# The turn from first to second stage of a two-level Strassen-Winograd kernel: where C11's last tile is squared, and where the first small product's sums stand

## The chip, the cores and the metric

The kernel runs on one core of one Trainium2 chip. The metric is the device time of one execution in microseconds (us), taken as a median of runs. The engines are called PE (TensorE's matmuls; PEld is its weight loads), DVE (VectorE), ACT (ScalarE), POOL (GpSimd) and SP (SyncE, which issues most transfers).

## The reference

```python
kv  = einsum('bhsd,bhse->bhde', k, v)           # 8 batches, 8 heads, 576 rows, 64 wide
out = einsum('bhsd,bhde->bhse', q, kv)
rms = sqrt(mean(out * out, axis=-1) + 1e-06)
x   = (out / rms * g_norm), heads side by side   # 4608 x 512
h   = x @ w_in                                   # w_in 512 x 2048
r   = maximum(h, 0)
g   = s * (r * r) + b                            # s, b scalars
return g @ w_out                                 # w_out 2048 x 512
```

All is float32. Linear attention without a softmax makes x. Two large products with the activation s * relu(h)^2 + b between them make nearly all of the work.

## The kernel before

The 4608 rows are worked through in nine **units** of 512 rows. In each unit the first stage computes h and the activation g, and the second stage computes g times w_out. Beside the two stages the attention of the next unit is computed, cut in pieces ("turn", "product", "back", "square", "row_sum", "norm", "turn_x", "scale") for two halves A and B of the unit. A dictionary tells after which step of the stages each piece is issued: `first` for numbered points in the first stage, `second` for points in the second. `at(n)` issues the pieces of point n.

Both products are done by the Strassen-Winograd scheme: each matrix is cut in 2 x 2 blocks, and seven products of sums of blocks take the place of eight. The seven are numbered 1 to 7. Products 1, 6, 5, 3 accumulate one after the other in one PSUM bank ("x"), 7 and 4 in another ("y"), 2 in a third ("z"); between two of them the bank's state is copied or added out. Unit 0 works without the scheme in its first stage, unit 1 with one level of it. Units 2 to 8, seven units, are **deep**: here some products are again cut into seven small ones. Only the deep units are touched by the change.

In a deep unit the first stage is `mm1_deep`, and `run` is its order, written out by hand. The columns of h come in four steps s = 0 to 3 (NS = 4). The blocks of g are a11 (also called C11), a12, a21, a22; each has one tile of 128 x 512 elements for each step, and two tiles of consecutive steps make a pair. `x1(s)`, `x6(s)`, `x5(s)`, `x3(s)`, `y7(s)`, `y4(s)` are the products of step s with what takes their results out. `small(i, pair, ...)` does the small products of products 2 and 3, whose results are added into a11 and a21. A tile becomes g by relu, square and affine (times s, plus b):

- `relu_sq_on_act(t)` does all three on ACT (lines 652, 653, 644), and `done(name, s)` calls it for a finished tile.
- `relu_sq(t, False)` does relu and square in one instruction on DVE (line 647); the affine on ACT follows by `scaled(name, s)` (line 644).

`s1(s)` adds tiles of a21 and a22 to a block "s1", and `s3(s)` replaces a21 by a11 minus a21; the second stage uses both as blocks.

The second stage is `mm2`, and `rest` is its order. Each of its seven products is cut again: `at_two_levels` makes, for a group of products, the functions `sums` (sums of quarters of g, on DVE, with numbers 5, 6, 7, 3 for the small products that use them), `go` (the matmuls of one small product), `out_of` (what takes its result out of PSUM) and `do` (go, then out_of). So `do_1(6)` is the small product 6 of product 1, A11 B11. Small product 1 needs no sum, since it reads a quarter of a11 as it is. Its result is copied by `keep` into r on DVE (`plus_of`, line 1087, with `nc.vector.tensor_copy`), and small product 6 then accumulates into the same bank; so it waits for this copy. Line 91 is the helper that issues every matmul, lines 250 and 253 the helpers for every DVE add and subtraction, so that in the profile these are told apart by the names of the tiles: "sub" is a sum for the second stage, "a" a tile of g.

Around the change the order on PE is: small(2,1,3,4), y4(2), x5(3), do_1(1), x3(3), y4(3), do_1(2), do_1(6), go_1(7), do_1(5), do_25(1), do_1(3), do_1(4), do_25(2), do_25(6), go_25(7), do_25(5). Every engine works its own instructions in the order in which the program issues them, and semaphores hold an instruction until what it needs is there. `x3(3)`, `y4(3)`, `s1(3)` and `s3(3)` belong to the first stage, but are handed to `rest` in the dictionary `last`, to be done there. Before the change `rest` begins after the call `sums()` of `run`, which zeroes two pieces of the output tile on POOL (`start_5`, line 1330) and makes the sums 5, 6 and 3 of product 1.

The x banks are two, taken in turn, and the y banks too. The DVE copy r has one buffer of its size.

Of the kernel before, what the change touches and what calls it, by code (L numbers as in the profile page):

```python
# [16 lines left out]
def kernel(  # L17
# [773 lines left out]
    def mm1_deep(u):  # L791
# [120 lines left out]
            for s in steps:  # L912
                relu_sq_on_act(ga[name, s])

        def run(at, early, sums):
            x1(0)
            at(2)
            x1(1)
            sums_of_x()
            small(2, 0, 1, 2)  # L920
            x6(0)
            at(4)
            y7(0)
            small(2, 0, 6, 7)
            at(5)
            x5(0)
            small(2, 0, 5)
            a22(0)
            at(6)
            x6(1)  # L930
            scaled("a22", 0)
            small(2, 0, 3, 4)
            at(7)
            y4(0)
            at(8)
            y7(1)
            done("a11", 0, 1)
            at(9)
            x5(1)
            scaled("a12", 0)  # L940
            a22(1)
            at(10)
            x1(2)
            small(3, 0, 1, 2)
            at(11)
            x1(3)
            scaled("a22", 1)
            y4(1)
            at(12)
            small(3, 0, 6, 7)  # L950
            y7(2)
            at(13)
            small(3, 0, 5)
            x6(2)
            scaled("a12", 1)
            at(14)
            small(3, 0, 3, 4)
            x6(3)
            done("a21", 0)
            at(15)  # L960
            small(2, 1, 1, 2)
            x5(2)
            done("a21", 1)
            s1(0)
            s3(0)
            at(16)
            small(2, 1, 6, 7)
            a22(2)
            scaled("a22", 2)
            y7(3)  # L970
            s1(1)
            small(2, 1, 5)
            x3(2)
            s3(1)
            small(2, 1, 3, 4)
            early()
            at(18)
            done("a11", 2)
            y4(2)
            s1(2)  # L980
            x5(3)
            done("a11", 3)
            scaled("a12", 2)
            a22(3)
            sums()
            s3(2)

        last = dict(
            x3=lambda: x3(3), y4=lambda: y4(3), x3_s1=lambda: s1(3), x3_s3=lambda: s3(3),
            y4_square=lambda: None,  # L990
        )
        return run, last
# [71 lines left out]
    def mm2(u, step=None, side={}):  # L1064
# [297 lines left out]

        def rest():
            do_1(1)
            step["x3"]()
            step["y4"]()
            do_1(2)
            step["y4_square"]()
            do_1(6)
            step["x3_s1"]()  # L1370
            go_1(7)
            do_1(5)
            sums_25((5, 6), 2)
            sums_25((7,), 5)
            at(0)
            do_25(1)
            do_1(3)
            sums_25((5, 6), 5)
            do_1(4)
            do_25(2)  # L1380
            at(1)
            step["x3_s3"]()
            s2((0,))
            do_25(6)
            s2((1,))
            sums_25((3,))
            go_25(7)
            s2((2,))
            do_25(5)
            s2((3,))  # L1390
            sums_6(())
            do_6(1)
            sums_6((5, 6))
            at(2)
            do_25(3)
            sums_6((7, 3))
            do_25(4)
            if end:
                for j in range(2):
                    store("o1", j, 4 * u + j, left, queues)  # L1400
            s4((0,))
            do_6(2, 6)
            s4((1, 2, 3))
            go_6(7)
            do_6(5)
            sums_73((5, 6), 7)
            sums_73((), 3)
            go_73(1)
            with_5(0, cols[0])
            out_73(1)  # L1410
            do_6(3)
            with_5(0, cols[1])
            sums_73((5, 6), 3)
            do_6(4)
            with_5(1)
            do_73(2)
            sums_73((7,))
            at(3)
            do_73(6)
            sums_73((3,))  # L1420
            at("sums")
            go_73(7)
            do_73(5)
            sums_4((5, 6))
            do_4(1)
            at(4)
            do_73(3)
            with_7(0)
            sums_4((7, 3))
            go_73(4, 7)  # L1430
            out_73(4, slice(0, 1))
            with_7(1)
            if end:
                for j in range(2):
                    store("o2", j, 4 * u + 2 + j, right, queues)
                store("o1", 0, 4 * u, right, queues)
            else:
                store("o1", 0, 4 * u, queues=queues)
            do_4(2, 6)
            go_4(7)  # L1440
            do_4(5)
            at(5)
            go_73(4, 3)
            out_73(4, slice(1, 2))
            if end:
                store("o1", 1, 4 * u + 1, right, queues)
            else:
                store("o1", 1, 4 * u + 1, queues=queues)
            do_4(3)
            at(6)  # L1450
            if end:
                store("o2", 0, 4 * u + 2, left, queues)
            else:
                store("o2", 0, 4 * u + 2, queues=queues)
            do_4(4)
            if end:
                store("o2", 1, 4 * u + 3, left, queues)
            else:
                store("o2", 1, 4 * u + 3, queues=queues)

        return {
            "early": lambda: (sums_1((7,)), sums_25((7,), 2)),
            "sums": lambda: (start_5(), sums_1((5, 6, 3))),
            "rest": rest,
        }

# [178 lines left out]
    def sides(u, A, B):  # L1645

        first, second = {}, {}
        kv = []  # L1650
        if u in kv_due:
            kv.append(lambda: kv_product(kv_due[u], u > 2))
            kv.append(lambda: used(*((u, "kv", (n, m)) for n in range(NP) for m in range(2))))
        q = {half: [partial(loads, u + 2, half)] for half in range(2)}
        if u == 1:
            for s in range(1, NS):
                first[((0, 1), (0, 3), (1, 1))[s - 1]] = list(sums_w_in(s))
            first.update({
                (1, 3): kv,
                (2, 0): [partial(A["turn"], 0), partial(A["turn"], 1)],  # L1660
                (2, 1): [A["product"]],
                (2, 2): [A["back"]],
                (2, 3): [A["square"]],
                (3, 0): [A["row_sum"]],
                (3, 2): [A["norm"], A["turn_x"]],
                (3, 3): [lambda: [load() for load in load_q(12, rest_on=nc.sync)]],
            })
            return first, second
        if u + 1 == U:
            return first, second  # L1670
        if u == 2:
            first = {
                4: [A["turn"]],
                5: kv,
                8: [A["product"]],
                9: [A["back"], B["turn"]],
                10: [A["square"]],
                11: [A["row_sum"]],
                12: [B["product"]],
                13: [A["norm"]],  # L1680
                14: [A["turn_x"]],
                15: [B["back"], *q[0]],
                18: [B["square"]],
            }
            second = {
                0: [B["row_sum"]], 1: [A["scale"]], 2: [B["norm"]], 3: [B["turn_x"], *q[1]],
                "sums": [B["scale"]],
            }
        else:
            first = {  # L1690
                2: [A["turn"]],
                4: [A["product"], *kv],
                5: [A["back"]],
                6: [A["square"], B["turn"]],
                7: [A["row_sum"]],
                8: [A["norm"]],
                9: [A["turn_x"]],
                10: [B["product"], *q[0]],
                11: [B["back"], A["scale"]],
                12: [B["square"]],  # L1700
                13: [B["row_sum"]],
                14: [B["norm"]],
                15: [B["turn_x"], *q[1]],
            }
            second = {1: [B["scale"]]}
        second[5], second[6] = [[lambda n=n: x_sums(u + 1)[n]()] for n in range(2)]
        return first, second

    for u in range(U):
# [4 lines left out]
        else:  # L1714
# [4 lines left out]
            if u > 1:  # L1719
                run, last = mm1_deep(u)  # L1720
                second = mm2(u, last, at_second)
                run(lambda n: [fn() for fn in first.get(n, [])], second["early"], second["sums"])
                second["rest"]()
                continue
            steps = [mm1(u, s) for s in range(NS)]
# [77 lines left out]
```

## Time and profile before

| | before |
|---|---|
| time, median of 3 runs | 915.05 us (914.61 to 915.32) |
| span of the profiled execution | 913.3 us |
| granted TensorE clock, mean | 1.000 |
| PE, share of the span in which it is busy | 99% |
| DVE, ACT, POOL | 73%, 40%, 25% |
| L647, relu and square on DVE, 128x512 | 54 instructions, 692 ns each |
| L652 and L653 on ACT, in place, 128x512 | 56 and 74 instructions, 621 and 630 ns each |
| L644, affine on ACT, 128x512 | 144 instructions, 812 ns each |
| L253, subtraction on DVE, 128x512 | about 685 ns each |
| L1087, copy r on DVE, 128x128 | 14 instructions, 288 ns each |

A line of the profile's groups names line, engine, operation, the tiles written and read, their shape, and how often it ran. A line of the timeline gives the start in us, the time until the group's end, the engine, the line and the tiles; in square brackets stands how long the engine had been idle before, and what released it. A line of the waits gives who waited for whom: in total, how many times, and the longest, in us. The ends of matmuls are modelled in the trace, their starts are not.

### The profile page before, as it was taken

What the parts mean: (1) busy time and instruction counts of PE and PEld (TensorE: products, weight loads), DVE (VectorE), ACT (ScalarE), POOL (GpSimd) and SP (SyncE); (2) the same over time, 40 slices, a digit from 0 to 9 for tenths busy, and PEclk for the clock granted to TensorE, in tenths of its full rate; (3) what the DMA queues carried; (4) which work ended last, traced back from release to release, by engine and by line L of the source; (5) the groups of instructions that cost most, each with busy time, mean ns of one, the idle gap of its engine ahead of it and who ended that gap; (6) DMA issues with size and microseconds to landing.
All of it is one profiled execution on the core that took longest, in us unless ns stands there. A gap on an engine that the chain in (4) does not pass through costs nothing. (4 is left out here: it accounts for less than half of the span.)

```text
span 913.3 us, 19278 instructions
## 1 busy us (share of the span) xinstructions
PE 899.8 (99%) x7522; PEld 826.3 (90%) x7522; DVE 662.4 (73%) x1223; ACT 364.3 (40%) x614; POOL 228.3 (25%) x432
## 2 busy tenths in 40 slices
PE   7999999999999999999999999999999999999998
PEld 6888888888888998999899998999899988999898
DVE  2898377587567986788677857785879778874686
ACT  2895134522148115630465026701680057204710
POOL 2000017014623233801283026503440300021000
PEclk9999999999999999999999999999999999999999
DMA  9698938239943994379536972598439811891286
GB/s 256 223 312 262 260 83 241 83 95 393 330 132 83 280 325 140 83 239 315 185 74 189 303 257 66 125 311 255 122 96 288 280 38 53 272 306 47 55 254 185
DMA packets 120138, 180.34 MB, mean 197 GB/s; under 512 B 29168, under 2 KB 46320, under 8 KB 120048
## 3 DMA queue, kind: packets, MB, share of 16 engines
q1 hardware_dynamic: 101552, 153.00, 53.6%
q0 software_dynamic: 15040, 23.88, 9.0%
q10 hardware_dynamic: 3456, 2.23, 1.0%
q8 instruction: 60, 0.98, 0.4%
q14 instruction: 30, 0.25, 0.1%
HBM read 153.36 MB, written 25.69 MB: 196 GB/s over the span
## 5 line engine op out<-in xcount | busy, mean ns | idle before, releaser
L1617 POOL DMA_DIRECT2D q_sb<-in_q_dram x256 | 144.1, 571 | 134.8 <-ACT a L652 62.5
L1206 POOL DMA_DIRECT2D out_dram<-o x110 | 55.0, 506 | 400.2 <-issue 154.5
L91 PE MATMUL x_ps<-w_sb,sub 128*128 128x128 f32 x1176 | 149.4, 276 | 3.1 <-DVE r L1087 2.9
L91 PEld LDWEIGHTS x_ps<-w_sb,sub 128*128 128x128 f32 x1176 | 139.7, 192 | 4.6 <-DVE r L1087 4.2
L644 ACT ACTIVATE a<-a,b_col,s_col 128x512 f32<-128x512 f32 x144 | 116.2, 812 | 29.4 <-DVE a L647 23.2
L91 PE MATMUL x_ps<-xs,ws 128*128 128x256 f32 x512 | 121.4, 380 | 0.1
L91 PE MATMUL y_ps<-xs,wb 128*128 128x256 f32 x512 | 120.8, 381 | 0.0
L91 PEld LDWEIGHTS y_ps<-xs,wb 128*128 128x128 f32 x512 | 94.6, 190 | 12.4 <-issue 0.6
L91 PEld LDWEIGHTS x_ps<-xs,ws 128*128 128x128 f32 x512 | 93.8, 190 | 11.7 <-ACT r L713 0.5
L814 ACT COPY a<-x_ps 128x512 f32<-128x512 f32 x28 | 16.4, 585 | 216.2 <-PE x_ps L91 216.0
L91 PE MATMUL x_ps<-xT,wa 128*128 128x256 f32 x384 | 89.0, 381 | 0.1
L91 PEld LDWEIGHTS x_ps<-xT,wa 128*128 128x128 f32 x384 | 71.3, 190 | 10.9 <-issue 1.3
L250 DVE TENSOR_TENSOR r<-sx_ps,a 128x256 f32<-128x256 f32 x63 | 26.6, 422 | 62.1 <-PE sx_ps L91 61.9
L91 PE MATMUL x_ps<-w_sb,a 128*128 128x128 f32 (+1 forms) x432 | 64.9, 298 | 0.0
L91 PE MATMUL y_ps<-w_sb,a 128*128 128x128 f32 (+1 forms) x416 | 62.1, 295 | 0.0
L91 PEld LDWEIGHTS x_ps<-w_sb,a 128*128 128x128 f32 x432 | 58.9, 191 | 3.3 <-issue 0.4
L91 PEld LDWEIGHTS y_ps<-w_sb,a 128*128 128x128 f32 x416 | 56.1, 192 | 2.1
L250 DVE TENSOR_TENSOR r<-x_ps,o 128x256 f32<-128x256 f32 (+1 forms) x84 | 29.7, 354 | 32.7 <-PE x_ps L91 30.6
L91 PE MATMUL y_ps<-w_sb,sub 128*128 128x128 f32 x392 | 49.5, 275 | 0.0
L253 DVE TENSOR_TENSOR a<-a,a 128x512 f32<-128x512 f32 x72 | 47.4, 684 | 0.4
L653 ACT ACTIVATE a<-a 128x512 f32<-128x512 f32 x74 | 46.7, 630 | 2.4
L91 PE MATMUL z_ps<-w_sb,a 128*128 128x128 f32 (+1 forms) x352 | 46.8, 280 | 0.0
(185 smaller groups left out, 1504.5 us busy)
## 6 DMA issues: line engine op xcount, KB each, us to landing
w_sb<-w SPq DMA_DIRECT2D x385, 256.0 KB, 4.6
w_raw<-in_moe_w_in_dram SPq DMA_DIRECT2D x8, 1024.0 KB, 6.1
w_raw<-in_moe_w_out_dram SPq DMA_DIRECT2D x8, 1024.0 KB, 5.0
w_sb<-w SPq DMA_DIRECT2D x14, 512.0 KB, 8.9
w<-sub POOLq DMA_DIRECT2D x28, 256.0 KB, 6.6
w_sb<-in_k_dram SPq DMA_DIRECT2D x24, 288.0 KB, 4.8
w_sb<-in_v_dram SPq DMA_DIRECT2D x24, 288.0 KB, 4.9
out_dram<-o POOLq DMA_DIRECT2D x92, 64.0 KB, 4.0
```

Source lines behind the costliest of these rows:

```text
L91: nc.tensor.matmul(o, lhsT=lhsT, rhs=rhs, start=start, stop=stop, skip_group_check=True)
L250: nc.vector.tensor_tensor(out=o, in0=a, in1=b, op=ALU.add)
L253: nc.vector.tensor_tensor(out=o, in0=a, in1=b, op=ALU.subtract)
L644: nc.scalar.activation(t, t, AF.Identity, scale=s_col, bias=b_col)
L653: nc.scalar.square(t, t)
L814: nc.scalar.copy(g_tile("a11", s), st["x", s])
L1206: queues[s % 2].dma_start(out=view[b, jj, :, cols], in_=st[name, j][s * w : s * w + w, cols])
L1617: load()
```

## The change

At the turn between the stages four things are done otherwise, in each of the seven deep units.

1. The last tile of C11, a11[3], gets relu and square from DVE (`relu_sq(ga["a11", 3], False)`), right after the small products that complete it. ACT does only the affine (`scaled("a11", 3)` in the place of `done("a11", 3)`). It is meant to have the tile ready earlier, and to take work off ACT.
2. The first small product of A11 B11, do_1(1), and its copy out of PSUM are issued ahead of start_5 and of the sums of product 1. It is meant to free the bank for do_1(6) earlier.
3. Of the sums of product 1, number 3 moves behind do_1(6). The difference s3(2) moves out of the turn to where s3(3) is, behind do_25(2).
4. In unit 2 alone, B's square (on ACT) moves from point 18 of the first stage to point 0 of the second, and B's row sum (on DVE, with a root on ACT) from point 0 to point 1, "a square of attention later".

No matmul is added, removed or moved.

```diff
--- before.py
+++ after.py
@@ -912,7 +912,7 @@
             for s in steps:
                 relu_sq_on_act(ga[name, s])
 
-        def run(at, early, sums):
+        def run(at, early):
             x1(0)
             at(2)
             x1(1)
@@ -973,20 +973,19 @@
             x3(2)
             s3(1)
             small(2, 1, 3, 4)
+            relu_sq(ga["a11", 3], False)
             early()
             at(18)
             done("a11", 2)
             y4(2)
             s1(2)
             x5(3)
-            done("a11", 3)
+            scaled("a11", 3)
             scaled("a12", 2)
             a22(3)
-            sums()
-            s3(2)
 
         last = dict(
-            x3=lambda: x3(3), y4=lambda: y4(3), x3_s1=lambda: s1(3), x3_s3=lambda: s3(3),
+            x3=lambda: x3(3), y4=lambda: y4(3), x3_s1=lambda: s1(3), x3_s3=lambda: (s3(2), s3(3)),
             y4_square=lambda: None,
         )
         return run, last
@@ -1362,11 +1361,14 @@
 
         def rest():
             do_1(1)
+            start_5()
+            sums_1((5, 6))
             step["x3"]()
             step["y4"]()
             do_1(2)
             step["y4_square"]()
             do_1(6)
+            sums_1((3,))
             step["x3_s1"]()
             go_1(7)
             do_1(5)
@@ -1460,7 +1462,6 @@
 
         return {
             "early": lambda: (sums_1((7,)), sums_25((7,), 2)),
-            "sums": lambda: (start_5(), sums_1((5, 6, 3))),
             "rest": rest,
         }
 
@@ -1680,10 +1681,9 @@
                 13: [A["norm"]],
                 14: [A["turn_x"]],
                 15: [B["back"], *q[0]],
-                18: [B["square"]],
             }
             second = {
-                0: [B["row_sum"]], 1: [A["scale"]], 2: [B["norm"]], 3: [B["turn_x"], *q[1]],
+                0: [B["square"]], 1: [B["row_sum"], A["scale"]], 2: [B["norm"]], 3: [B["turn_x"], *q[1]],
                 "sums": [B["scale"]],
             }
         else:
@@ -1719,7 +1719,7 @@
             if u > 1:
                 run, last = mm1_deep(u)
                 second = mm2(u, last, at_second)
-                run(lambda n: [fn() for fn in first.get(n, [])], second["early"], second["sums"])
+                run(lambda n: [fn() for fn in first.get(n, [])], second["early"])
                 second["rest"]()
                 continue
             steps = [mm1(u, s) for s in range(NS)]
```

## The prediction

> **What bounds the kernel now.** I read the page's busy times first, then the waits of TensorE and of its weight loads, then the timeline round the turn in the last unit and in unit 2, and last the chain of waits.
>
> ```profile
> PE 899.8 (99%) x7522; PEld 826.3 (90%) x7522; DVE 662.4 (73%) x1223; ACT 364.3 (40%) x614; POOL 228.3 (25%) x432
> ```
> TensorE (PE) is never long without work, so the time changes only by what PE does or by the moments in which it stands. The change leaves its instructions and their order as they are; only the moments are left. All of PE's waits come to under 10 us; one kind comes in every deep unit:
>
> ```profile
> PE x_ps L91 <- DVE r L1087: 2.9, 7, 0.4
> PE x_ps L91 <- ACT a L827: 0.4, 1, 0.4
> PEld x_ps L91 <- DVE r L1087: 4.2, 7, 0.6
> PEld x_ps L91 <- ACT a L827: 0.6, 1, 0.6
> ```
> (Total us, times, longest.) Seven times, once in each of the units 2 to 8, a product into an x bank waits for the VectorE copy "r" of line 1087. The single wait for ACT at line 827 lies in unit 2. The last unit's timeline (start, length, engine, line) shows the cause:
>
> ```profile
> 862.08 0.63 ACT L652 ACTIVATE a<-a 128x512 f32<-128x512 f32 x1
> 862.74 0.63 ACT L653 ACTIVATE a<-a 128x512 f32<-128x512 f32 x1
> 863.41 1.52 ACT L644 ACTIVATE a<-a,b_col,s_col 128x512 f32<-128x512 f32 x2
> 864.25 0.69 DVE L250 TENSOR_TENSOR sub<-a,a 128x512 f32<-128x512 f32 x1 [1.34 <-ACT a L644]
> 865.70 0.69 DVE L253 TENSOR_TENSOR sub<-a,sub 128x512 f32<-128x512 f32 x1
> 865.79 1.05 PE L91 MATMUL z_ps<-w_sb,a 128*128 128x128 f32 x8
> 866.31 0.68 DVE L253 TENSOR_TENSOR a<-a,a 128x512 f32<-128x512 f32 x1
> 866.92 0.28 DVE L1087 COPY r<-x_ps 128x128 f32<-128x128 f32 x1
> 867.25 1.16 PE L91 MATMUL x_ps<-w_sb,sub 128*128 128x128 f32 x8 [0.41 <-DVE r L1087]
> 868.25 1.06 PE L91 MATMUL y_ps<-w_sb,sub 128*128 128x128 f32 x8
> ```
> ACT needs relu, square and affine for C11's last tile, so the first sum (5) starts on VectorE only at 864.25, after 1.34 us idle. Three sums and s3(2) then stand ahead of the copy of the small product do_1(1), which PE had ended by 862.29. The next product into that bank, do_1(6), waits for that copy.
>
> How much is one wait? PE's ends are modelled, so I count starts. Eight such matmuls take 0.89 us from start to start where nothing waits:
>
> ```profile
> 885.39 0.89 PE z_ps L91 x8
> 886.28 0.89 PE x_ps L91 x8
> ```
> From do_1(2) (865.79) to go_1(7) (868.25) there are two such groups: 2.46 us where 1.78 would do. **The loss is 0.68 us a unit**, of which the wait's label shows 0.41 and the start after it (1.16 for 1.05) 0.11; 7 x 0.68 = 4.76 us.
>
> **The Trainium skill.** "Perfetto Trace Analysis", Per-instruction lifecycle, says that the reported end of a TensorE instruction is estimated from its size; hence starts. The trace agrees: labels of 0.41 (PE) and 0.60 (PEld) for a shift of 0.68. "TensorE: Matmul & The Clock Gate", Part 2, step by step, says that only weight loads are pulled ahead and matmuls stay in program order, so what stands behind do_1(6) waits with it; here even its weight load stood. "PSUM — Partial Sum Buffer", Engine vs sequencer instructions, calls VectorE's and ScalarE's queues strict FIFO: the copy was behind the sums although its product had long ended, as the trace shows.
>
> **The change, part by part**, in the last unit's clock.
>
> *Square of C11's last tile on VectorE.* It adds one L647 instruction (692 ns) per unit behind the last add of small(2,1,...), at 858.14, and removes one L652 and one L653 (0.66 us of ACT each, by their starts). In a full queue 128x512 instructions follow each other at 0.60, one that needs its predecessor at 0.73 (859.87 to 860.60). So: square 858.60, the two early differences 859.21 and 859.81, the add of y4(2) 860.45 (was 859.87), its square 861.18, s1(2) 861.79, the add of a22(3) 862.39 to 863.08 (was 862.22 to 862.91, there held by ACT's copy). Nobody on PE waits for these before y4(3), which needs the y bank that a22(3) reads; its weights load at 863.85, so 0.77 is left. Cost on the path: none. ACT's affine of a11[3] comes right behind its copy for x5(3), at 862.08, and ends at 862.89 instead of some 864.2.
>
> *The copy of do_1(1) ahead of the sums.* It follows a22(3)'s add: 863.00 to 863.29. Sum 5 starts at 863.2, sum 6 at 863.93, ending at 864.62. do_1(6) needs the copy and sum 6, and is due at 866.68 after x3(3), y4(3), do_1(2): **2 us to spare**, so the wait goes whole.
>
> *Sum 3 after do_1(6).* do_1(6) ends about 867.57, its copy runs 867.77 to 868.06, sum 3 to 868.75; do_1(3) needs it at 871.14. do_1(5), due 868.46, needs that copy (0.4 to spare) and sum 5. Hidden.
>
> *s3(2) to later.* It joins s3(3) behind the add of do_25(2), 0.60 us ahead of the copy of do_25(6), for which do_25(5) waits. In unit 5: add 689.43, then s3(2) 689.77, s3(3) 690.37, s2(0) 690.97, copy 691.57 (was 691.27, after 0.22 idle) to 691.99; do_25(5) loads at 692.69. The rest of the delay ends at VectorE's next idle time, 0.69 ahead of 694.79. Cost nothing, with 0.7 to spare.
>
> *The memsets of start_5.* GpSimd ran them at 671.40 in unit 5, nine microseconds ahead of need. Nothing.
>
> *Unit 2's attention.* The square moves from the turn to point 0, the row sum from 0 to point 1. Before:
>
> ```profile
> 285.09 1.04 ACT L564 ACTIVATE xn<-q_sb 128x1024 f32<-128x1024 f32 x1
> 288.69 1.99 PE L91 MATMUL x_ps<-xT,ws 128*128 128x256 f32 x8 [0.40 <-ACT a L827]
> 299.74 1.21 DVE L568 TENSOR_REDUCE ss<-xn 128x16 f32<-128x1024 f32 x1
> 304.26 0.42 DVE L250 TENSOR_TENSOR r<-x_ps,o 128x256 f32<-128x256 f32 x1
> 314.79 1.16 PE L91 MATMUL x_ps<-w_sb,sub 128*128 128x128 f32 x8 [0.25 <-DVE r L250]
> ```
> The square held up ACT's copy for x5(3), and x3(3) waited. From do_1(1) to y4(3) unit 2 takes 3.29 us (287.23 to 290.52), the last unit 2.67 (861.40 to 864.07): **0.62 us gained**. At point 0 ACT is otherwise idle (3.41 us before 300.99), so there the square is free. The row sum is not: it now stands between the add of do_25(2) and the copy for which do_25(5) waits. In unit 2's old clock: add 302.05, row sum 302.39, s3(2) 303.52, s3(3) 304.12, s2(0) 304.72, copy 305.32 to 305.74. do_25(5) was due at 305.33 (weights): some 0.44 with the start after it. VectorE then has 0.35 idle to take up and stays 0.6 behind until the copy at 314.45, where PE waits already; that wait ends 0.6 later. It contains the first loss: **0.6 us lost in all** (bounds: 0, if VectorE is early enough; 1.2, the whole row sum).
>
> Sum: 4.76 + 0.62 - 0.60 = 4.8 us. 915.05 - 4.8 = **910.3 us**.
>
> **Rivals.**
> 1. *Half given back.* VectorE's later queue is tighter than I read (0.4 at do_1(5), 0.7 at do_25(5)): 0.3 lost in each unit, 7 x 0.3 = 2.1, gives 912.4. For it: the row sum shows that a single long instruction there reaches PE. Against: both places end in idle VectorE.
> 2. *The wait is replaced.* do_1(6) or do_1(5) waits for the copy or a sum as long as before, in every unit: only unit 2 changes, by nothing net: 915.1. Against: 2 us to spare.
> 3. *Slower.* Both VectorE pieces, 0.69 for the square and 0.68 for s3(2), reach PE in full, at y4(3) and do_25(5): 7 x 1.37 = 9.6 lost, 4.8 gained: 919.9. For it: VectorE is full from 857 to 861. Against: it waits 1.34 us for ACT soon after, and 0.77 is left at y4(3).
>
> **How the numbers follow.** Forecast 0.70, rival 1 0.15, rival 2 0.08, rival 3 0.07. The range holds the first two. Low end: unit 2 loses nothing, 915.05 - 4.76 - 0.62 = 909.7, less 0.4 for the spread of the times before (914.61 to 915.32): 909.3. High end: each wait worth only its label, 7 x 0.41 + 0.40, less 1.2 for the row sum, is 2.1 gained: 913.0. Faster 0.85, same 0.08, slower 0.07.
>
> **What would show it.** The seven waits for r of line 1087 gone from PE and PEld; do_1(2) to go_1(7) 1.78 us. Line 647 with 61 instructions for 54; in-place line 652 with 49 for 56, line 653 with 67 for 74. Sum 5 about 1 us earlier in the unit, right behind the copy. In unit 2 y4(3) 2.67 us after do_1(1), and a new wait for r of line 250 near 305. Wrong would make it: a wait of y4(3) for line 250's add, of do_25(5) in every unit, or of do_1(5) for the copy ahead of it.

## The result and the profile after

| | before | changed |
|---|---|---|
| time, median of 5 runs | 914.82 us (914.61 to 915.32) | 910.59 us (910.17 to 910.77) |
| ratio to before, 95% interval | | 0.9952 [0.9937, 0.9966] |
| the same in a second comparison (5 runs, 9 of before) | 914.97 us | 910.16 us, 0.9946 [0.9934, 0.9959] |
| span of the profiled execution | 913.3 us | 908.9 us |

The kernel became faster by 4.2 us in one comparison and by 4.8 in the other. The first line of the page after, with the busy times:

```profile
PE 897.7 (99%) x7522; PEld 825.3 (91%) x7522; DVE 664.5 (73%) x1230; ACT 356.0 (39%) x600; POOL 228.1 (25%) x432
```
PE has the same 7522 instructions. DVE has seven more, ACT fourteen fewer: the squares of C11's last tile. Busy shares hardly move; the time came out of PE's waits, which I read next (PE, all kinds; total us, times, longest):

```profile
PE kv_ps L366 <- DMA kv_sb<-in_v_dram: 2.4, 3, 1.2
PE xT_ps L473 <- DVE xn L455: 1.5, 1, 1.5
PE warm_ps L91 <- POOL ident masks.py:199: 1.4, 1, 1.4
PE x_ps L91 <- DVE r L250: 0.6, 2, 0.4
PE x_ps L91 <- DVE qT L421: 0.5, 1, 0.5
PE y_ps L91 <- DVE inv L453: 0.4, 1, 0.4
PE y_ps L91 <- DVE wb L245: 0.3, 1, 0.3
```
The seven waits for r of line 1087 and unit 2's wait for ACT at line 827 are gone. One has come: r of line 250 was waited for once, now twice. The rest lies in unit 0 or in the loading ahead of it and differs from execution to execution. The timeline of the last unit's turn (line 1087 is now 1086):

```profile
854.86 0.69 DVE L647 SCALAR_TENSOR_TENSOR a<-a 128x512 f32<-128x512 f32 x1
857.65 1.05 PE L91 MATMUL x_ps<-w_sb,a 128*128 128x128 f32 x8
858.34 1.52 ACT L644 ACTIVATE a<-a,b_col,s_col 128x512 f32<-128x512 f32 x2
858.60 0.68 DVE L250 TENSOR_TENSOR a<-y_ps,a 128x512 f32<-128x512 f32 x1
859.20 0.28 DVE L1086 COPY r<-x_ps 128x128 f32<-128x128 f32 x1
859.40 0.68 DVE L250 TENSOR_TENSOR sub<-a,a 128x512 f32<-128x512 f32 x1
862.05 1.05 PE L91 MATMUL z_ps<-w_sb,a 128*128 128x128 f32 x8
862.94 1.06 PE L91 MATMUL x_ps<-w_sb,sub 128*128 128x128 f32 x8
863.84 1.06 PE L91 MATMUL y_ps<-w_sb,sub 128*128 128x128 f32 x8
```
DVE squares a11[3]; do_1(1) starts on PE at 857.65; ACT does the affine alone; the copy of do_1(1) follows a22(3)'s add, and sum 5 follows the copy without idle time. From do_1(2) (862.05) to go_1(7) (863.84) it is 1.79 us, within the trace's rounding of the 1.78 of two groups without a wait. It is so in all seven units.

I call **unit 2's length** the time from the start of its do_1(1) to that of unit 3's. The starts of such groups on PE, read from the timelines, give this table, with which every kernel below is read:

| kernel | do_1(2) to go_1(7) | unit 2: do_1(1) to y4(3) | unit 2: go_25(7) to do_25(5) | unit 2's length |
|---|---|---|---|---|
| before | 2.46 | 3.29 | 1.78 | 97.81 |
| changed | 1.78 | 2.67 | 2.16 | 97.12 |
| square only | 1.78 | 3.29 | 1.78 | 97.10 |
| order only | 1.78 | 3.29 | 1.78 | 97.81 |
| attention only | 2.46 | 2.67 | 1.78 | 97.19 |
| attention undone | 1.79 | 3.29 | 1.79 | 97.10 |
| row sum in the gap | 1.78 | 2.67 | 1.79 | 96.48 |
| sums not split | 1.78 | 2.67 | 1.79 | 96.53 |
| copy of do_25(6) late | 1.78 | 2.67 | 3.36 | 98.15 |
| y bank late | 1.78 | 3.20 | 1.79 | 97.16 |

Over the whole span: unit 2's do_1(1) started 0.23 us later in the changed profile (287.46 for 287.23). This delay is already there in unit 0, which the change doesn't touch: a product that starts at 27.71 us before starts at 27.98 in the changed profile. From unit 2's do_1(1) to unit 8's it took 3.98 us less (570.19 for 574.17), and the rest after that was 0.65 shorter. That is the 4.4 us between the two spans.

### The profile page after: what moved, and what is told of

Same layout as the page of the kernel before. It is cut to its first block, busy times and chain, and to the rows that moved or that the text cites. A ratio compares the mean times of both kernels' runs of the same rounds, so it can differ in the third digit from the quotient of the medians.

```text
span 908.9 us, 19257 instructions
## 1 busy us (share of the span) xinstructions
PE 897.7 (99%) x7522; PEld 825.3 (91%) x7522; DVE 664.5 (73%) x1230; ACT 356.0 (39%) x600; POOL 228.1 (25%) x432
## 3 DMA queue, kind: packets, MB, share of 16 engines
q10 hardware_dynamic: 3456, 2.23, 1.0%
## 4 chain that ended last, share of the span: by engine, by line
PE 93%; DVE 4%; DMA 1%; ACT 1%; issue 0%; SPq 0%; DVEq 0%
PE x_ps L91 48%; PE y_ps L91 28%; PE z_ps L91 9%; PE sx_ps L91 4%; PE y_ps L545 2%; DMA kv_sb<-in_v_dram 1%; PE kv_ps L366 1%; PE z_ps L366 1%; DVE xn L578 0%; DVE a L253 0%; PE y_ps L366 0%; DVE sub L253 0%; DVE o L250 0%; DVE xs L253 0%; PE qT_ps L534 0%
## 5 line engine op out<-in xcount | busy, mean ns | idle before, releaser
L250 DVE TENSOR_TENSOR a<-y_ps,r 128x512 f32<-128x512 f32 x36 | 24.7, 687 | 35.2 <-PE y_ps L91 29.7
```

Of the source, the lines that this page charges most:

```text
L250: nc.vector.tensor_tensor(out=o, in0=a, in1=b, op=ALU.add)
```

## The experiments

The theory: TensorE waited in each unit because VectorE came to the copy of do_1(1) too late, and what ends this wait is any way of bringing VectorE there earlier. The rivals: only the order does it, or only the square, or both are needed; and VectorE's work that was added or moved holds TensorE up elsewhere.

**Square only.** Of the change, this alone:

```diff
             small(2, 1, 3, 4)
+            relu_sq(ga["a11", 3], False)
             early()
...
-            done("a11", 3)
+            scaled("a11", 3)
```


> The kernel before with only the square of C11's last tile on VectorE and its affine alone left to ACT; the sums 5, 6, 3 and s3(2) still stand ahead of the copy of do_1(1), and unit 2's attention is where it was. Theory (the wait is a matter of when VectorE gets to the copy, and either part alone brings it early enough): sum 5 starts about 1.25 us earlier, since a22(3)'s add now ends at 863.08 and ACT's affine at 862.89 in the last unit's old clock; 6, 3, s3(2) follow at 863.7, 864.4, 865.1, the copy ends at 865.96, 0.7 before do_1(6) is due at 866.68. All seven losses of 0.68 us go: 914.8 - 4.8 = 910.0. Unit 2 keeps its 0.62 us wait of x3(3) for ACT. Rival 1 (the order alone does it, the square only takes work off ACT): the copy stays behind four instructions and do_1(6) still waits, near 914.5. Rival 2 (the added VectorE work reaches PE): 0.3 to 0.7 lost a unit at y4(3), 912 to 915.

Measured: 910.43 us, ratio 0.9949 [0.9936, 0.9963], and do_1(2) to go_1(7) 1.78 us in all units. Its last unit:

```profile
857.44 1.05 PE L91 MATMUL x_ps<-w_sb,a 128*128 128x128 f32 x8
858.99 0.68 DVE L250 TENSOR_TENSOR sub<-a,a 128x512 f32<-128x512 f32 x1
861.03 0.69 DVE L253 TENSOR_TENSOR a<-a,a 128x512 f32<-128x512 f32 x1
861.63 0.28 DVE L1088 COPY r<-x_ps 128x128 f32<-128x128 f32 x1
862.73 1.06 PE L91 MATMUL x_ps<-w_sb,sub 128*128 128x128 f32 x8
```
The copy is still behind the sums and s3(2), but sum 5 starts 1.55 us after do_1(1) where it was 2.85, so the copy ends at 861.91 and do_1(6) starts at 862.73 without waiting. The theory held: within the spread of the runs the square by itself brings all that the change brings (910.16 us for the changed kernel on the same chip).

**Order only.** do_1(1) ahead of start_5 and the three sums, all else as before:

```diff
-            sums()
             s3(2)
...
             do_1(1)
+            start_5()
+            sums_1((5, 6, 3))
             step["x3"]()
```


> The kernel before with only the order changed: do_1(1) and its copy ahead of start_5 and the sums 5, 6, 3; s3(2) stays in the first stage's order, now ahead of the copy; ACT still does relu, square and affine of C11's last tile; unit 2's attention is where it was. Theory (either part alone suffices): the copy follows s3(2) and ends at about 863.7 in the last unit's old clock; sum 5 still starts at 864.25, when ACT's affine is done, sum 6 ends at 865.7, 1 us before do_1(6) is due: all seven losses go, 914.8 - 4.8 = 910.0. Rival 1 (do_1(6) really waits for its sum, and the copy is only the last of two): the wait becomes one for sum 6 and stays half or more of what it was, 912.5 to 914.5. Rival 2 (both parts are needed): about 912.5.

Measured: 911.98 us, ratio 0.9966 [0.9953, 0.9978]. The wait of do_1(6) is gone in all units (1.78), as the theory said, but the kernel is 1.5 us slower than with the square only, and none of the three expected times fits. Its last unit shows one part of this:

```profile
865.71 1.06 PE L91 MATMUL x_ps<-w_sb,sub 128*128 128x128 f32 x8
867.40 0.81 ACT L644 ACTIVATE a<-a,b_col,s_col 128x512 f32<-128x512 f32 x1
868.12 0.24 ACT L1086 COPY r<-x_ps 128x128 f32<-128x128 f32 x1
868.40 0.29 DVE L250 TENSOR_TENSOR o<-y_ps,r 128x128 f32<-128x128 f32 x1 [1.49 <-ACT r L1086]
868.42 1.16 PE L91 MATMUL x_ps<-w_sb,sub 128*128 128x128 f32 x8
```
do_1(5) starts at 865.71. Its result is copied by ACT, which is still busy with relu, square and affine of a12's last tile, because it did those of a11's before; the copy ends at 868.36, and do_1(3), which goes on in the same bank, was due at 868.39. It starts at 868.42 with a slow first group (1.16 for 1.06): 0.13 us lost in each unit, 0.9 in all, and the waits do not list it. In unit 2 the row sum at point 0 also makes VectorE late for both halves of do_25(6); the second half waits for its sum:

```profile
299.76 1.21 DVE L568 TENSOR_REDUCE ss<-xn 128x16 f32<-128x1024 f32 x1
301.94 0.69 DVE L253 TENSOR_TENSOR sub<-sub,s 128x512 f32<-128x512 f32 x1
302.68 1.16 PE L91 MATMUL x_ps<-w_sb,sub 128*128 128x128 f32 x8 [0.17 <-DVE sub L253]
```
From do_25(2)'s second group to go_25(7) it is 3.25 us for 2.68: 0.57 lost. 4.76 - 0.92 - 0.57 = 3.3 us of gain, and 3.1 were measured. So the square on VectorE has a second use with this order: it takes 1.25 us off ACT ahead of the copy of do_1(5). In the changed kernel, which has both, this copy ends at 866.09, 1.3 us before do_1(3) starts (867.41). In the kernel before ACT was as late as here, but TensorE came 0.68 us later too.

**Attention only**, in the kernel before:

```diff
-                18: [B["square"]],
...
-                0: [B["row_sum"]], 1: [A["scale"]], 2: [B["norm"]], 3: [B["turn_x"], *q[1]],
+                0: [B["square"]], 1: [B["row_sum"], A["scale"]], 2: [B["norm"]], 3: [B["turn_x"], *q[1]],
```


> The kernel before with only unit 2's attention moved: B's square to point 0 of the second stage, B's row sum and root to point 1. Theory: unit 2's do_1(1) to y4(3) falls from 3.29 to 2.67 us (0.62 gained); without s3(2) beside it the row sum ends early enough, the copy of do_25(6) ends at about 305.1 in unit 2's old clock where do_25(5) loads at 305.33, and only some 0.1 is lost at do_6(5). 914.8 - 0.5 = 914.3; the waits for the copy r of line 1087 stay seven. Rival (the row sum alone costs what the square gains): a wait of do_25(5) of 0.4 or more, 914.8.

Measured: one run at 914.76 us, too few to show half a microsecond; the trace has to. The seven waits are unchanged. The profile's unit 2 began 0.27 us later than before's, and takes 97.19 us for 97.81: the 0.62 of the square are won and nothing is lost to the row sum, which without s3(2) beside it lets the copy end in time. The theory held; of its 0.1 at do_6(5) at most 0.03 showed.

**Attention undone**, in the changed kernel: the same lines the other way.

> The changed kernel with unit 2's attention put back: B's square at point 18 of the first stage, B's row sum at point 0 of the second. Theory: unit 2 loses its 0.62 us again at x3(3), and gets back about 0.3 of the 0.6 us that it lost at do_25(5) and do_6(5), for the row sum still ahead in VectorE's queue leaves some of it: about 910.9 where the changed kernel has 910.6; no wait of do_25(5) or one under 0.1. Rival (moving the attention is what made the change pay in unit 2): 911.3 or more.

Measured: one run at 910.77 us. y4(3) in unit 2 is late again by 0.62, but do_25(5) is not, and unit 2 takes 97.10 us for the changed kernel's 97.12. I had expected 0.3 of the loss to be won back and it was 0.64. Beside the other parts of the change, moving the attention is worth nothing: unit 2 wins 0.62 and pays as much.

**Row sum in the gap**, in the changed kernel:

```diff
             do_1(4)
+            at("gap")
             do_25(2)
...
-                0: [B["square"]], 1: [B["row_sum"], A["scale"]],
+                0: [B["square"]], "gap": [B["row_sum"]], 1: [A["scale"]],
```


> The changed kernel with unit 2's row sum issued between do_1(4) and do_25(2), where VectorE stood idle for 0.99 us waiting for do_25(2), in place of behind do_25(2). Theory (the changed kernel loses in unit 2 what the moved square gains, because the row sum and s3(2) together stand ahead of the copy for which do_25(5) waits): the row sum starts as soon as the add of do_1(4) is out and ends nearly when do_25(2) does, the copy of do_25(6) comes about 1 us earlier, do_25(5) waits no more (go_25(7) to do_25(5) 1.79 us for 2.16), and the wait of do_6(5) goes back to 0.25. Unit 2's first small product to unit 3's takes 96.5 us for 97.12; 910.6 - 0.6 = 910.0. Rival (the row sum takes the time wherever it stands, since VectorE has no idle time there that later work does not use): 97.1, 910.6.

The changed kernel in unit 2, and then this one:

```profile
300.99 0.42 DVE L250 TENSOR_TENSOR o<-z_ps,r 128x256 f32<-128x256 f32 x1 [0.99 <-PE z_ps L91]
301.33 1.21 DVE L568 TENSOR_REDUCE ss<-xn 128x16 f32<-128x1024 f32 x1
304.26 0.42 DVE L250 TENSOR_TENSOR r<-x_ps,o 128x256 f32<-128x256 f32 x1
304.73 2.05 PE L91 MATMUL x_ps<-w_sb,sub 128*128 128x128 f32 x16 [0.21 <-DVE r L250]
314.34 1.16 PE L91 MATMUL x_ps<-w_sb,sub 128*128 128x128 f32 x8 [0.35 <-DVE r L250]
```
```profile
299.60 1.21 DVE L568 TENSOR_REDUCE ss<-xn 128x16 f32<-128x1024 f32 x1
300.73 0.42 DVE L250 TENSOR_TENSOR o<-z_ps,r 128x256 f32<-128x256 f32 x1
302.86 0.42 DVE L250 TENSOR_TENSOR r<-x_ps,o 128x256 f32<-128x256 f32 x1
304.04 1.95 PE L91 MATMUL x_ps<-w_sb,sub 128*128 128x128 f32 x16
```
The row sum fills the 0.99 us in which VectorE waited for do_25(2). Counted from do_25(6)'s start (300.79 in the changed kernel, 300.47 here) the copy of do_25(6) (302.86) starts 2.39 us after it for 3.47, and do_25(5) (304.04) starts on time. The label of do_6(5)'s wait, 0.35 in the changed kernel, is 0.24 again. Unit 2 takes 96.48 us, as expected. The time was 909.49 us, ratio 0.9939 [0.9926, 0.9951]. Beside the changed kernel on one chip:

> The changed kernel, unaltered, on the same chip as the next. Theory: 910.6 us, ratio to the kernel before 0.995; unit 2's first small product to unit 3's 97.1 us, go_25(7) to do_25(5) in unit 2 2.16 us.

> The changed kernel with unit 2's row sum between do_1(4) and do_25(2), beside the changed kernel itself. Theory (0.64 us is won in unit 2 and nothing elsewhere): 0.6 us less than the changed kernel, unit 2's first small product to unit 3's 96.5 us for 97.1. Rival (the 1.1 us between the two medians so far is a difference of the whole kernel): 1 us or more less. Rival (it was a difference between two chips): none.

Measured: 910.16 and 909.45 us, 0.7 apart; unit 2's lengths 97.12 and 96.47. The gain is unit 2's. The intervals of the two ratios to the kernel before overlap (0.9946 [0.9934, 0.9959] and 0.9941 [0.9928, 0.9955]). What tells the two apart is the traces, and the times of the single runs on that chip (909.88 to 910.27, and 909.32 to 909.94), which overlap by only 0.06 us. It is the fastest version that I have.

**Sums not split**, in the changed kernel: its third part undone.

```diff
             a22(3)
+            s3(2)
...
-            sums_1((5, 6))
+            sums_1((5, 6, 3))
...
-            sums_1((3,))
```
with s3(2) taken from behind do_25(2).

> The changed kernel with its third part undone: sums 5, 6 and 3 together behind the copy of do_1(1), and s3(2) back in the turn, ahead of that copy. The square on VectorE, do_1(1) ahead of the sums and unit 2's attention stay. Theory (the third part gains nothing, and s3(2) behind the row sum is half of what unit 2 loses): do_1(2) to go_1(7) stays 1.78 us in all units, do_25(5) in unit 2 waits no more or under 0.1, unit 2's first small product to unit 3's takes about 96.6 for 97.12; 910.6 - 0.5 = 910.1. Rival (s3(2) and sum 3 had to leave the turn for the wait to go): the wait for the copy or the sum comes back, 912 or more.

Measured: 909.78 us, ratio 0.9942 [0.9928, 0.9955]; no wait comes back at the turn, and unit 2 takes 96.53 us. The third part of the change won nothing. And with s3(2) gone from behind the row sum, the copy of do_25(6) starts 2.87 us after do_25(6) for 3.47, and nearly the whole loss of unit 2 is gone, as it was with the row sum gone from ahead of s3(2): either alone fits into VectorE's spare time there, the two together do not.

**Copy of do_25(6) late**, a test of the 0.7 us to spare:

```diff
-            s2((0,))
+            s2((0, 1, 2))
             do_25(6)
```
with the later `s2((1,))` and `s2((2,))` left out.

> The changed kernel with two VectorE instructions that stand behind the copy of do_25(6), s2(1) and s2(2), put ahead of it; nothing added. Theory (0.7 us to spare at do_25(5), and 0.60 us for each 128x512 instruction in a full queue): the copy ends 1.2 us later, so do_25(5) comes 1.79 + 0.42 + 0.11 = about 2.3 us after go_25(7) in units 3 to 8 and 3.3 in unit 2, which had no spare time; 6 x 0.53 + 1.2 = 4.4 lost, 915.0. Rival (there is far more spare time than read, or do_25(5) waits for something else): no change, 910.6. Rival (there is none): 7 x 1.2 = 8.4 lost, 919.

Measured: 914.73 us, ratio 0.9996 [0.9988, 1.0004]. do_25(5) comes 2.23 us after go_25(7) in units 3 to 8, and 3.36 in unit 2, which had nothing to spare:

```profile
877.93 0.42 DVE L250 TENSOR_TENSOR r<-x_ps,o 128x256 f32<-128x256 f32 x1
878.40 2.05 PE L91 MATMUL x_ps<-w_sb,sub 128*128 128x128 f32 x16 [0.28 <-DVE r L250]
```
The 0.44 and 0.11 more at the next group make 0.55 a unit where 0.53 was expected, and 915.0 us was expected for the whole. So the 0.7 us to spare were real, and two VectorE instructions in a wrong place are enough to eat up nearly the whole gain.

**y bank late**, a test of the 0.77 us left at y4(3):

```diff
             s1(2)
+            g_s1(2)
+            s3(2)
```
with s3(2) taken from behind do_25(2).

> The changed kernel with two VectorE instructions of 128x512 ahead of a22(3)'s add: s1(2) done twice (the second time writes the same values again) and s3(2), which is taken from behind do_25(2). Theory (0.77 us were left at y4(3) with the square on VectorE, and the square itself cost nothing there): the add ends 1.2 us later, y4(3) comes 0.2 to 0.3 us late in each unit, 7 x 0.25 = 1.8 lost; unit 2 wins about 0.5 since s3(2) no longer stands behind the row sum: 911.9. Rival (VectorE's queue is tight at the turn, so that every instruction added there reaches TensorE): 7 x 1.2 = 8.4 lost, 918.5. Rival (there is more than 1.2 to spare): 910.1.

Measured: 914.21 us, ratio 0.9991 [0.9982, 0.9999], 2.3 us above what I expected. y4(3) comes 0.53 us late in every unit; with the next group the loss is 0.63. Last unit:

```profile
860.52 1.05 PE L91 MATMUL x_ps<-w_sb,a 128*128 128x128 f32 x8
860.86 1.41 DVE L250 TENSOR_TENSOR s<-a,a 128x512 f32<-128x512 f32 x2
862.38 0.69 DVE L253 TENSOR_TENSOR a<-a,a 128x512 f32<-128x512 f32 x1
862.99 0.68 DVE L250 TENSOR_TENSOR a<-y_ps,a 128x512 f32<-128x512 f32 x1
863.72 1.99 PE L91 MATMUL y_ps<-xs,wb 128*128 128x256 f32 x8 [0.37 <-DVE a L250]
```
The add of a22(3) starts 2.47 us after do_1(1), in the changed kernel 0.95: my two instructions took 1.52 us, not 1.20. I had priced them at 0.60 each as if they were independent. But the second s1(2) writes what the first wrote, and s3(2) changes a tile that it read; the three start 0.72 and 0.80 apart. With 1.52 the spare time is nearly what was read: in the changed kernel the add ended at 859.28 and y4(3)'s weights loaded at 860.11, 0.83 later, and 1.52 - 0.83 = 0.69 where 0.63 was lost. Unit 2 won some 0.6 back, about as expected, since do_25(5) is on time there (1.79), so that it takes 97.16 us for the changed kernel's 97.12.

## Why the prediction was right

910.3 us was forecast and 910.59 and 910.16 were measured: a gain of 4.8 us, and gains of 4.2 and 4.8. The 0.6 between the two is no more than the spread of the single runs (0.7 us before, 0.6 us in the changed kernel).

- *A loss of 0.68 us a unit, seven times.* Right: do_1(2) to go_1(7) fell from 2.46 to 1.78 us in every unit. Had I taken the label of the wait (0.41), I would have forecast 2.9 in place of 4.8 us.
- *VectorE's queue with the square in it.* Counted from do_1(1), a22(3)'s add was put at +0.99 and came at +0.95; the copy at +1.60 and came at +1.55. No wait of y4(3).
- *Two microseconds to spare at do_1(6), and the rest of the moves hidden.* Right in units 3 to 8, which have no new wait. (The times in the prediction that are put in unit 5, 671.40 and 689.43 to 694.79, are those of unit 6, whose do_1(1) starts at 675.23; the reading holds for it.) The prediction credits the end of the wait to the new place of the copy and did not ask which part was needed. The experiments answer it: the square alone suffices; the order alone ends this wait but makes do_1(3) late, which needs ACT's copy. The prediction did not look at that copy. That it has 1.3 us to spare in the changed kernel comes from the square; for the forecast it was luck. The place where I had seen 0.4 us to spare, do_1(5), showed no wait.
- *Unit 2: 0.62 won, 0.60 lost.* Both were right: 2.67 for 3.29 us at the turn, and 0.61 lost by the lengths (0.68 + 0.62 less the 0.69 by which unit 2 became shorter). do_25(5) was put at 0.44 and lost 0.48 (0.37, and 0.11 at the next group); do_6(5), where the prediction put the rest, lost 0.10 more than before.
- *Rivals.* Half given back, the wait replaced, slower: all three would have shown as a wait in units 3 to 8, and there is none. They were not far off: two more VectorE instructions ahead of do_25(5)'s copy or of y4(3)'s add give 914.7 and 914.2 us.

## What to carry to other kernels

Price a wait of TensorE by the starts of the groups around it, against the same groups where nothing waits; in every case here the label was too small. When an engine's queue is late, ask which single instruction ahead of the waited-for one starts late and why: here it was ACT's three passes over one tile, and handing two of them to the engine that was idle waiting for them was worth more (4.7 us) than moving the copy ahead of the sums (3.1 us). And when a piece of side work is moved off one queue, look for the next engine's idle time just ahead of a wait for TensorE, and put it there, not just behind it.

## What was not expected of the hardware

- A wait of TensorE cost its label and about a quarter of a microsecond more: 0.41 cost 0.68 (before, do_1(6)), 0.28 cost 0.55 (copy late, do_25(5)), 0.37 cost 0.63 (y bank late, y4(3)), 0.21 cost 0.48 (changed, unit 2), and 0.40 cost 0.62 (before, unit 2's x3(3)). The traces show where this comes from. Undisturbed groups follow each other at 0.89 us but are listed with 1.06, so the label, which is counted from the modelled end, leaves out the first 0.17; and the next group comes another 0.05 to 0.11 late. So a loss can have no label at all (order only, do_1(3): 0.03 late, and 0.10 more at the next group).
- In a full queue VectorE starts independent 128x512 instructions every 0.60 us though each lasts 0.68 to 0.69. Where one works on the tile that its predecessor has just written it is 0.72 to 0.73 (sum 5 at 859.40 and sum 6 at 860.12 in the changed kernel's last unit). A chain in a queue is a fifth longer than its count says. The 0.80 of y bank late, between the second s1(2) and s3(2), is more than that: s1(0) and s3(0), which also follow each other, are 0.73 apart in the same trace. What makes the difference is open.
